# An attention and gated feed-forward kernel on one core: LayerNorm sums of one block moved to ScalarE, a new start, a new schedule, and the last store in two parts

## The chip, the core and the metric

The kernel runs on one core of one Trainium2 chip. The metric is device time in microseconds (us), quoted as the median of a kernel's runs; lower is better. The profiled span is shorter than the time of the same run by about 1.7 us (560.1 and 561.8 for the kernel before), so spans are compared with spans and times with times.

## The reference, cut to what matters

```python
S, D, H, W, F = 2048, 576, 32, 256, 4608          # one sequence, bf16
xn = layernorm(x)                                 # no scale, no shift, eps 1e-5
q, k, v = split(xn @ wqkv)                        # 32 heads of 18
s = softmax(where(0 <= i - j < W, q k^T * 18**-0.5, -1e9)) v @ wo
h = sigmoid(xn @ w_gate) * (xn @ w_up)            # 576 -> 4608
g = silu(h @ w_down)                              # 4608 -> 576
return x + s * g
```

## The kernel before

A Python program lists operations with engine, estimated duration and dependencies. A list scheduler then orders them per engine, using those estimates alone. So a constant in an estimate moves instructions without changing any of them. The sequence is worked off in four chunks of 512 tokens. The parts that matter:

```python
NTAIL = 96
NWARM = (11, 4, 1)                   # warm-up pairs of 512 columns
PARTS = (((0, 1), (1, 2), (2, 3), (3, 4)),) * 2   # first two feature tiles: block by block of 128 tokens
SPACE_NS = 1500.0                    # least distance of two score groups
BLOCKS = (range(KB), range(1, KB))   # KB = 5: block 0 is the 64-row remainder of D = 576, first in its turn

def turn(eng, outs, lhs, rhs, hi):   # half of a product: first half hi=0, second half hi=1 (array halves swapped)
    for k in BLOCKS[hi]:
        res = pair(eng, outs, ..., not hi and k == 0, bool(hi) and k == KB - 1, hi)

def dve_ns(n, rate=1.0):             # estimate for VectorE
    return n / (0.96 * rate) + 140.0

# LayerNorm of block i (build_ln)
b1 = op("DVE", 390, ... bn_stats(columns 0:288));  b2 = op("DVE", 390, ... bn_stats(columns 288:576))
ag = op("DVE", 200, ... bn_aggr);  ve = op("DVE", 140, ... add EPS)
rs = op("POOL", 560, ... pow(-0.5))
ap = op("DVE", 430, ... (x - mean) * rstd);  dup = op("DVE", 180, ... copy of 64 columns)
# ... transposes on TensorE, copy out of PSUM on ScalarE (blocks 0 to 2) or VectorE (block 3)

# last block of the last chunk: 192 columns a half first, then the narrow group of NTAIL a half
self.build_final(sb + 1, hs[1], fa, 0, na)
self.build_final(sb + 1, ht, down(i + 1, ht, 1, [lb], 2 * na, NTAIL), 2 * na, NTAIL)
...
if c0 + w == D:                      # one store of 128 x 576 when both parts are ready
    o = self.dma(self.out[rows, :], self.xf[:, sx, :], ...)

# the sync queue, when the program is written out
for o in self.prog[e]:
    if e == "SP" and o is self.prog[e][-1]:     # ahead of its last DMA
        for i, n in enumerate(lane_cnt):
            if n > 0 and i not in outs:
                eng.wait_ge(lanes[i], n)        # every DMA lane but the output's: 31 instructions in the trace
```

The softmax here doesn't subtract the row's maximum and nothing guards it: scores larger than these inputs give would overflow.

Of the kernel before, what the change touches and what calls it, by code (L numbers as in the profile page):

```python
# [38 lines left out]
TURN_NS = 290.0  # L39
# [6 lines left out]
BINS0 = (((-4, 0, 1), (1, 1, 5), (6, 6, 2)),  # L46
         ((-2, 2, 1), (3, 3, 5)),
         ((0, 0, 5), (5, 5, 3)),
         ((2, 2, 5), (7, 7, 1)),
         ((4, 4, 4),))  # L50
MASKS0 = (((0, 2, 0, 2),), ((2, 1, 0, 2), (7, 1, 0, 1)), ((0, 1, 1, 2), (4, 1, 0, 2)), ((2, 1, 1, 2), (6, 1, 0, 2)), ((4, 1, 1, 2),))
# [6 lines left out]
NTAIL = 96  # L58
NWARM = (11, 4, 1)
NEARLY = 2  # L60
FIRST_SLACK_NS = -970.0
PARTS = (((0, 1), (1, 2), (2, 3), (3, 4)),) * NEARLY
XPRIO = 0
# [6 lines left out]
SHARE_NS = 300.0  # L70
# [5 lines left out]
SPACE_NS = 1500.0  # L76
# [25 lines left out]
BLOCKS = (range(KB), range(1, KB))  # L102
# [10 lines left out]
def turn(eng, outs, lhs, rhs, hi):  # L113
    res = None
    for k in BLOCKS[hi]:
        res = pair(eng, outs, lambda r, t: lhs(r, t, k), lambda r, t: rhs(r, t, k), not hi and k == 0,
                   bool(hi) and k == KB - 1, hi)
    return res


def dve_ns(n, rate=1.0):
    return n / (0.96 * rate) + 140.0
# [54 lines left out]
class Op:  # L177
    __slots__ = ("eng", "est", "deps", "fn", "name", "prio", "start", "end", "tok", "needs_tok",
                 "nbytes", "slack", "idx", "succs", "cidx", "odeps", "acq", "lane", "filler")

    def __init__(self, eng, est, fn, name, deps, prio, nbytes, odeps, acq):
        self.eng = eng
        self.est = float(est)
        self.fn = fn
        self.name = name
        self.deps = []
        seen = set()
        stack = list(deps)
        while stack:
            d = stack.pop(0)  # L190
            if d is None:
                continue
            if isinstance(d, (list, tuple)):
                stack = list(d) + stack
            elif id(d) not in seen:
                seen.add(id(d))
                self.deps.append(d)
        self.prio = prio
        self.start = None
        self.end = None  # L200
        self.tok = None
        self.needs_tok = False
        self.nbytes = nbytes
        self.idx = -1
        self.succs = []
        self.cidx = -1
        self.odeps = [d for d in odeps if d is not None]
        self.acq = acq
        self.lane = None
        self.slack = 0.0  # L210
        self.filler = None
        for d in self.odeps:
            assert d.eng == eng
# [22 lines left out]
class Builder:  # L236
# [38 lines left out]
    def alloc_memory(self):  # L275
# [49 lines left out]
        self.small, _ = seq("small", [P, 3 + 16 * NST], f32)  # L325
# [4 lines left out]
        self.veps = sm[:, 3 + 14 * NST:3 + 15 * NST].rearrange("p (s c) -> p s c", c=1)  # L330
        self.rstd = sm[:, 3 + 15 * NST:3 + 16 * NST].rearrange("p (s c) -> p s c", c=1)
# [62 lines left out]
    def load_x(self, c, i=0):  # L394
        if c == 0:
            for i in range(BPC):
                self.x_dma[i] = (self.dma(self.x0[:, i, :], self.x[i * P:(i + 1) * P, :], P * D * 2, f"dma:x{i}", ("x0", i), prio=XPRIO * (i > 1)),
                                 self.x0[:, i, :])
                self.x_dma[i][0].slack = -220.0
            return  # L400
        st = c * BPC + i
        slots, dd = [], []
        for _ in range(2):
            s_, d_ = self.r_xr.produce()
            slots.append(s_)
            dd += d_
        assert slots[1] == slots[0] + 1
        o = self.dma(self.xr[:, slots[0]:slots[0] + 2, :],
                     self.x[st * P:(st + 2) * P, :].rearrange("(t p) d -> p t d", p=P),
                     2 * P * D * 2, f"dma:x{st}", ("x", slots[0]), deps=[dd, self.hm[6] if c == 1 else None], prio=5)  # L410
        o.slack = 5000.0
        for j in range(2):
            self.x_dma[st + j] = (o, self.xr[:, slots[j], :])
# [5 lines left out]
    def load_rem(self, dst, srcs, name, lane, prio, deps=()):  # L419
        return [self.dma(dst[ROWS[t], :], src[0:RD, :], RD * src.shape[1] * 3, name, lane + (t,), deps=deps, prio=prio)  # L420
                for t, src in enumerate(srcs)]

    def build_consts(self):
# [15 lines left out]
        self.warm(NWARM[0], z, None, 427)  # L439
# [12 lines left out]
        for t in range(2):  # L452
            for i in range(2):
                self.op_wqk4.append(op("DVE", 130, lambda e, t=t, i=i: e.tensor_copy(
                    self.wq4[ROWS[t], 0, i, :], self.wqkr[ROWS[i], 512:D]), f"init:wq4:{t}{i}", deps=self.op_wqk, prio=2))

    def warm(self, n, dep, before, est):
        h, zero = self.warm_h, self.warm_src

        def f_warm(eng):  # L460
            return pair(eng, self.halves(h, NT), lambda r, t: zero[r, :],
                        lambda r, t: zero[r, None, :].broadcast_to([SW, NT // P, P]), True, True)
# [29 lines left out]
    def build_ln(self, c):  # L492
# [3 lines left out]
        for i in range(BPC):  # L496
            st = c * BPC + i
            if c and i % 2 == 0:
                self.load_x(c, i)
            pr = 2 if c else (0, 3, 8, 8)[i]  # L500
            o_x, x_in = self.x_dma[st]
            ss, ds = self.r_st.produce()
            b1 = op("DVE", 390, lambda e, ss=ss, x_in=x_in: e.bn_stats(self.bnst[:, ss, 0, :], x_in[:, 0:288]),  # L503
                    f"ln:bn1:{st}", deps=[o_x, ds], prio=pr)
            b2 = op("DVE", 390, lambda e, ss=ss, x_in=x_in: e.bn_stats(self.bnst[:, ss, 1, :], x_in[:, 288:576]),  # L505
                    f"ln:bn2:{st}", deps=[o_x, ds], prio=pr)
            ag = op("DVE", 200, lambda e, ss=ss: e.bn_aggr(self.mv[:, ss, :], self.bnst[:, ss, :, :]),
                    f"ln:ag:{st}", deps=[b1, b2], prio=pr)
            ve = op("DVE", 140, lambda e, ss=ss: e.tensor_scalar(self.veps[:, ss, :], self.mv[:, ss, 1:2], EPS, None,
                                                                ALU.add), f"ln:ve:{st}", deps=[ag], prio=pr)  # L510
            rs = op("POOL", 560, lambda e, ss=ss: e.tensor_tensor(self.rstd[:, ss, :], self.veps[:, ss, :],
                                                                  self.neghalf[:, :], ALU.pow),
                    f"ln:rs:{st}", deps=[ve, self.op_negh], prio=pr)
            sn, dn = self.r_xn.produce()
            ap = op("DVE", 430, lambda e, ss=ss, x_in=x_in, sn=sn: e.tensor_scalar(  # L515
                self.xnr[:, sn, RD:XW], x_in, self.mv[:, ss, 0:1], self.rstd[:, ss, :],
                ALU.subtract, ALU.mult), f"ln:ap:{st}", deps=[rs, ag, dn], prio=pr)
            dup = op("DVE", 180, lambda e, sn=sn: e.tensor_copy(self.xnr[:, sn, 0:RD], self.xnr[:, sn, RD:2 * RD]),
                     f"ln:dup:{st}", deps=[ap], prio=pr)
# [16 lines left out]
            if i < 2:  # L536
                self.warm(NWARM[1 + i], None, tr, 216)

# [3 lines left out]
            eng = "DVE" if i == 3 else "ACT"  # L542
            xe = op(eng, dve_ns(KB * P, 1.9) if i == 3 else act_ns(KB * P), f_xe, f"xe:{st}", deps=[tr], prio=0)
            h.release(xe)
            self.op_xnT[c].append(xe)

# [111 lines left out]
    def build_attn(self, c, hg):  # L658
# [21 lines left out]
        for vi, (specs, groups) in enumerate(zip(bins, masks)):  # L680
# [15 lines left out]
            self.last_vis = sc  # L696
            vis.append(sc)
# [34 lines left out]
    def build_pv(self, c, pr):  # L732
# [5 lines left out]
        kss = [ks for ks in (0, 5, -4, -3, -2, -1, 1, 2, 3, 4, 6, 7) if c or ks >= 0]  # L738
# [25 lines left out]
        for i in range(2):  # L764
# [10 lines left out]
            rc = op("DVE", 200, lambda e, o1=o1: e.reciprocal(o1[:, :, DH], o1[:, :, DH]), f"rc:{c}:{pr}:{i}", deps=[t1], prio=1)  # L775
# [55 lines left out]
    def build_ffn(self, c):  # L831
# [17 lines left out]
        def weights(wg):  # L849
# [5 lines left out]
            if wg % 2 == 0:  # L855
# [4 lines left out]
                                                ("wgr", sr), pr, [dr])  # L860
            ds += self.op_wgr[wg - wg % 2]
            slots[wg] = sw
            wops[wg] = ds
            if c == 0 and wg == 0:
                for d in ds:
                    d.slack = FIRST_SLACK_NS
# [11 lines left out]
        def gate_up(ft, h, half, acq, part=None, deps=()):  # L878
# [8 lines left out]
            def f(eng):  # L887
                return turn(eng, [bank(h, w)[:, t0:t0 + n] for w in range(2)], lhs, lambda r, t, k: x_in[r, k, t0:t0 + n], half)
            o = op("PE", len(BLOCKS[half]) * mm_ns(n), f, f"f1{half}:{c}:{ft}", deps=[xin, wops[ft // WG], deps],
                   prio=3 if part is None else 1, odeps=chain[half] if part is None else [], acq=acq)  # L890
# [16 lines left out]
        early = NEARLY if c == 0 else 0  # L907
        if early:
# [3 lines left out]
            for ft, h in enumerate(hs):  # L912
                u = None
                for part in range(len(PARTS[ft])):
                    lo = gate_up(ft, h, 0, None if part else h, part, [u])
                    u = gate_up(ft, h, 1, None, part, [lo])
# [3 lines left out]
        for ft in range(early, NFT):  # L920
            if ft % WG == 0 and ft // WG not in slots:
                weights(ft // WG)
            h = self.pool_f.hold()
            lo = gate_up(ft, h, 0, h)
# [30 lines left out]
        for i in range(0, BPC, 2):  # L955
# [7 lines left out]
            ht = self.pool_s.hold()  # L963
# [5 lines left out]
            lb = down(i + 1, ht, 0, [], 2 * na, NTAIL)  # L969
            fa = down(i + 1, hs[1], 1, [la], 0, na, range(NFG - 1, NFG))  # L970
            self.build_final(sb + 1, hs[1], fa, 0, na)
            self.build_final(sb + 1, ht, down(i + 1, ht, 1, [lb], 2 * na, NTAIL), 2 * na, NTAIL)
        self.prev_f2_last = new_last

    def build_final(self, sb, h, f2, c0=0, n=288):
# [42 lines left out]
        if c0 == 0:  # L1018
            self.fq3 = []
        self.fq3.append(q3)  # L1020
        if c0 + w == D:
            o = self.dma(self.out[rows, :], self.xf[:, sx, :], P * D * 2, f"dma:out:{sb}", ("out", sx), deps=self.fq3, prio=2)
            self.r_xf.release(sx, o)

    def schedule(self):
# [14 lines left out]
        while nsched < len(ops):  # L1040
            best = None
            for e in ENGS:
# [4 lines left out]
                if e == "PE":  # L1047
                    for o in cand:
                        if o.acq is not None:
                            due = last_sc + SPACE_NS if o.name.startswith("sc") else 0.0  # L1050
                            claims.setdefault(o.acq.pool.name, []).append((o.prio, o.cidx, max(ready_t[o.cidx], due)))
                bk = None
                for o in cand:
                    st = max(free[e], ready_t[o.cidx])
                    early = 0.0
                    if e == "PE" and o.name.startswith("sc"):
                        early = min(max(0.0, last_sc + SPACE_NS - st), FILL_NS)
# [24 lines left out]
            if o.name.startswith("sc"):  # L1082
# [24 lines left out]
            for s_ in o.succs:  # L1107
# [8 lines left out]
                if remaining[s_.cidx] == 0:  # L1116
# [121 lines left out]
```

## Time and profile before

| | kernel before |
|---|---|
| time, three runs | 562.5 us (562.21 to 562.64) |
| profiled span | 560.1 |
| all matmuls but the warm-ups at their steady rates | 542.5 |
| first gate/up matmul | 7.87 |
| the 144 small (128-column) gate/up matmuls done | 12.89 |
| TensorE's last matmul ends | 556.27 |
| last store issued, landed | 557.89, 559.64 |

The table cuts the span into three: a start (to 12.89), a middle (12.89 to 556.27, 543.38 us), and an end (3.84 us).

### The profile page before, as it was taken

How to read it: one execution, taken by the hardware profiler on the slowest of the kernel's cores; microseconds unless marked ns; L12 is line 12 of the kernel's file. 1: busy time of each engine (PE TensorE's matmuls, PEld its weight loads, DVE VectorE, ACT ScalarE, POOL GpSimd, SP SyncE). 2: the span in 40 equal slices, each digit the busy share in tenths (PEclk: the TensorE clock that was granted, in tenths of full speed). 3: DMA queues.
4: the chain of work that ended last, by engine and by line, in shares of the span. 5: the costliest groups of instructions: out<-in, count | busy, mean ns of one | idle time of the engine just before them, and what ended most of it. 6: DMA issues, size and time to landing. Idle time of an engine off the chain costs nothing.

```text
span 560.1 us, 19180 instructions
## 1 busy us (share of the span) xinstructions
PE 553.5 (99%) x8300; PEld 335.7 (60%) x8300; DVE 335.7 (60%) x793; ACT 271.4 (48%) x379; POOL 210.8 (38%) x358
## 2 busy tenths in 40 slices
PE   8999999999999999999999999999999999999997
PEld 4454544677764454556877566555487754444786
DVE  5576879769587776734886773586656133333133
ACT  3245655545655656466655636665754133323011
POOL 4564467473366534405674530465330100000000
PEclk9999999999999999999999999999999999999999
DMA  8975899541215454427321243454521126552010
GB/s 230 319 216 153 241 279 261 154 59 35 76 37 155 133 143 144 116 75 128 97 58 35 81 116 98 125 157 125 164 66 36 32 70 176 166 161 57 1 44 23
DMA packets 113323, 67.81 MB, mean 121 GB/s; under 512 B 18476, under 2 KB 111372, under 8 KB 113240
## 3 DMA queue, kind: packets, MB, share of 16 engines
q1 hardware_dynamic: 105816, 60.68, 39.6%
q0 software_dynamic: 7424, 5.92, 3.9%
q8 instruction: 65, 1.06, 0.8%
q14 instruction: 18, 0.15, 0.1%
HBM read 55.15 MB, written 2.36 MB: 103 GB/s over the span
## 4 chain that ended last, share of the span: by engine, by line
PE 97%; DVE 2%; DMA 0%; issue 0%; DVEq 0%
PE ps L109 93%; PE ps L754 3%; DMA x<-in_A_x_dram 0%; DVE o2T L780 0%; DVE ot L772 0%; DVE small L503 0%; DVE s_attn L1005 0%; DVE small L505 0%; DVE o L776 0%; DVE thf L1010 0%; DVE v_aug L652 0%; DVE xnr L515 0%; PE ps L553 0%; DVE xf L1015 0%; DVE ot L775 0%
## 5 line engine op out<-in xcount | busy, mean ns | idle before, releaser
L109 PE MATMUL ps<-xnT,wgs 64*128 64x512 bf16 (+1 forms) x2400 | 285.6, 368 | 0.1
L704 ACT ACTIVATE expr<-ps 128x1024 bf16<-128x1024 f32 (+2 forms) x160 | 156.7, 979 | 86.6 <-PE ps L109 86.0
L109 PEld LDWEIGHTS ps<-xnT,wgs 64*128 64x128 bf16 x2400 | 113.8, 94 | 116.8 <-PE ps L109 0.9
L109 PE MATMUL ps<-wd_sb,hT 64*128 64x288 bf16 (+2 forms) x2448 | 154.3, 276 | 0.0
L900 DVE SCALAR_TENSOR_TENSOR hT<-tring,ps 128x512 bf16<-128x512 bf16 x144 | 98.0, 683 | 89.6 <-ACT tring L897 87.1
L897 ACT ACTIVATE tring<-ps 128x512 bf16<-128x512 f32 x144 | 85.9, 597 | 114.4 <-PE ps L109 112.7
L109 PEld LDWEIGHTS ps<-wd_sb,hT 64*128 64x128 bf16 x2448 | 113.1, 94 | 28.0
L265 POOL DMA_DIRECT2D qk<-qd x160 | 82.6, 524 | 106.6 <-PE ps L109 99.8
L717 DVE TENSOR_TENSOR expr<-expr,mask 128x256 bf16<-128x256 bf16 (+2 forms) x232 | 63.7, 305 | 53.2 <-ACT expr L704 52.5
L669 POOL TENSOR_SCALAR kx<-kprev,small 128x256 bf16<-128x256 bf16 x64 | 62.0, 979 | 31.5 <-PE ps L109 30.8
L265 POOL DMA_DIRECT2D oT<-o2T x72 | 36.9, 520 | 61.9 <-DVE o2T L780 50.0
L109 PE MATMUL ps<-qk,kx 64*128 64x320 bf16 (+4 forms) x736 | 59.8, 251 | 0.0
L109 PE MATMUL ps<-xnT,wgr 64*128 64x512 bf16 (+1 forms) x300 | 55.9, 368 | 0.3
L109 PEld LDWEIGHTS ps<-qk,kx 64*128 64x128 bf16 x736 | 32.0, 94 | 25.5 <-DVE hT L900 1.4
L109 PE MATMUL ps<-xnT,wqk 64*128 64x512 bf16 x256 | 32.6, 377 | 0.0
L772 DVE STREAM_TRANSPOSE ot<-ps 128x512 f32<-128x512 f32 x32 | 22.4, 701 | 13.4 <-PE ps L754 13.3
L995 ACT ACTIVATE thf<-ps 128x576 bf16<-128x576 f32 (+3 forms) x22 | 11.4, 519 | 36.3 <-PE ps L109 35.8
L591 DVE CAST qd<-ps 128x1024 bf16<-128x1024 f32 (+1 forms) x20 | 22.2, 1114 | 6.2 <-PE ps L109 5.9
L669 DVE TENSOR_SCALAR kx<-qk,small 128x512 bf16<-128x512 bf16 x64 | 22.2, 373 | 3.3 <-PE ps L109 3.1
L780 DVE STREAM_TRANSPOSE o2T<-o 128x512 bf16<-128x512 bf16 x32 | 22.8, 711 | 1.1
L109 PEld LDWEIGHTS ps<-xnT,wgr 64*128 64x128 bf16 x300 | 15.0, 94 | 13.8 <-issue 1.3
L825 ACT ACTIVATE s_attn<-ps 128x576 bf16<-128x576 f32 x16 | 9.9, 648 | 27.1 <-PE ps L109 27.1
(64 smaller groups left out, 301.9 us busy)
## 6 DMA issues: line engine op xcount, KB each, us to landing
wgs<-in_B_w_gate_dram SPq DMA_DIRECT2D x72, 256.0 KB, 3.4
wgs<-in_B_w_up_dram SPq DMA_DIRECT2D x72, 256.0 KB, 3.9
wd_sb<-in_B_w_down_dram SPq DMA_DIRECT2D x9, 576.0 KB, 6.4
qk<-qd POOLq DMA_DIRECT2D x100, 36.0 KB, 2.3
wgr<-in_B_w_gate_dram SPq DMA_DIRECT2D x36, 64.0 KB, 2.3
wgr<-in_B_w_up_dram SPq DMA_DIRECT2D x36, 64.0 KB, 2.4
xf<-in_A_x_dram SPq DMA_DIRECT2D x16, 144.0 KB, 2.7
out_dram<-xf SPq DMA_DIRECT2D x16, 144.0 KB, 1.8
```

The costliest lines, as they stand in the source:

```text
L109: res = eng.matmul(outs[i], lhs(ROWS[t], i), rhs(ROWS[t], i), start=start, stop=stop, tile_position=(64 * t, 0))
L265: o = self.op(eng, DMA_ISSUE_NS[eng], lambda e: e.dma_start(dst, src), name, deps, prio, nbytes=nbytes)
L591: return eng.tensor_copy(dst, self.both(h, n))
L669: return e.tensor_scalar(self.kx[:, sx, pos:pos + n_ // SW, t, :], src.rearrange("p (s k) -> p s k", k=SW), self.half[:, t:t + 1], None, A ...
L704: return eng.activation(self.expr[:, se, :, lo * SW:NT], self.both(h, NT)[:, :, lo * SW:NT], ACTF.Exp, scale=SM_SCALE)
L717: return eng.tensor_tensor(e_, e_, m_, ALU.mult)
L754: res = eng.matmul(outs[i][p0:p0 + VH, cols], self.v_aug[ROWS[i], o:o + VH], self.expr[ROWS[i], se, t, cols], start=n == 0, stop=n == len( ...
L772: return e.transpose(self.ot1[:, p1, :], self.halves(hp, NT)[i])
L780: t2 = op("DVE", dve_ns(NT), lambda e, p2=p2, p3=p3: e.transpose(self.o2T[:, p3, :], self.o2[:, p2, :]), f"ot2:{c}:{pr}:{i}", deps=[on, d3 ...
L897: th = op("ACT", act_ns(NT), lambda e: e.activation(self.tring[:, st, :], bank(h, 0), ACTF.Tanh, scale=0.5), f"th:{c}:{ft}", deps=[pg, dt_ ...
L900: mu = op("DVE", dve_ns(NT), lambda e: e.scalar_tensor_tensor(self.hT[:, ft, :], self.tring[:, st, :], 1.0, bank(h, 1), ALU.add, ALU.mult) ...
L995: return e.activation(v2(t)[:, a:b, :], y2()[:, a:b, :], ACTF.Tanh, scale=0.25)
```

## The change

The intent: shorten the start (ScalarE, idle there, takes the sums of block 2; short warm-ups; the remainder's weights last, so that the first turn waits for two loads only), drop the score columns of the first chunk that only meet keys before the sequence, give the scheduler numbers nearer to measured ones, and let the last block's first part be stored while the second is computed. The order of the P V products became a named list with the same content.

```diff
+STATS_ACT = (2,)
-NWARM = (11, 4, 1)
+NWARM = (43, 10)                       # pairs of 128 columns now
-NTAIL = 96
+NTAIL = 112
-BLOCKS = (range(KB), range(1, KB))
+BLOCKS = ((1, 2, 3, 4), (1, 2, 3, 4, 0))
-BINS0 = (((-4, 0, 1), (1, 1, 5), (6, 6, 2)), ((-2, 2, 1), (3, 3, 5)), ...)
+BINS0 = (((0, 0, 5), (5, 5, 3)), ((1, 1, 5), (6, 6, 2)), ...)   # no negative key blocks in chunk 0
-TURN_NS = 290.0
+TURN_NS = 265.0
-SHARE_NS = 300.0
+SHARE_NS = 0.0
-SPACE_NS = 1500.0
+SPACE_NS = ((1500, 1500, 1400, 1500, 2000, 1200, 2000, 1100), ...)   # per chunk and head group
-    return n / (0.96 * rate) + 140.0
+    return n / (0.96 * rate) + 160.0
@@ build_ln, block 2 of chunk 0
+        a1 = op("ACT", ..., activation(junk, x_in, Identity, accum_out=sx))
+        m  = op("POOL", ..., nm = sx * (-1 / D))
+        a2 = op("ACT", ..., activation(junk, x_in, Square, bias=nm, accum_out=sq))
+        v  = op("POOL", ..., ve = sq / D + EPS)
+        rs = op("POOL", ..., pow(-0.5))
@@ build_ffn, chunk 0
+   the first half turn of feature tile 2 (512 columns) is placed inside tile 1's last parts as filler
@@ build_final
-        if c0 + w == D:
-            o = self.dma(self.out[rows, :], ...)
+        if c0 == 0 or c0 + w == D:
+            a, b = self.out_from, c0 + w
+            o = self.dma(self.out[rows, a:b], ...)
```

(Cut: the reciprocal's estimate 200 to 255, slacks and priorities of loads, mask tables, bookkeeping.)

## The prediction

> **What bounds the kernel now.** I read the page's engine shares first, then the chain of waits, then the start, one middle stretch and the end in the timeline, because the page already says that the middle is full.
>
> ```profile
> span 560.1 us, 19180 instructions
> PE 553.5 (99%) x8300; PEld 335.7 (60%) x8300; DVE 335.7 (60%) x793; ACT 271.4 (48%) x379; POOL 210.8 (38%) x358
> PE 97%; DVE 2%; DMA 0%; issue 0%; DVEq 0%
> ...
> 24.14 2.75 PE L109 MATMUL ps<-xnT,wqk 64*128 64x512 bf16 x24
> 26.73 0.38 PE L109 MATMUL ps<-xnT,wgr 64*128 64x512 bf16 x2
> ```
>
> TensorE is busy 99% and is 97% of the chain. Busy alone could hide slow matmuls, so I check the rate: 24 matmuls of 512 columns run as 12 pairs (two 64-row halves of the array at once), and the next group starts 26.73 - 24.14 = 2.59 us later, 0.216 us a pair. I did this for every group, from the start times of the 8300 matmuls: 0.216 us a pair at 512 columns, 0.123 at 288, 0.056 at 128, 0.028 at 64. Counting all matmuls but the warm-ups at these rates (P V as eight at a time) gives 542.5 us. The rest of the 560.1 us is what any change to the schedule can win: 7.87 us before the first gate/up matmul, 3.84 us after the last matmul, and some 6 us of small holes between[...].
>
> The start (timeline of TensorE, VectorE):
>
> ```profile
> 1.05 3.90 PE L109 MATMUL ps<-hT 64*128 64x512 bf16 x22 [1.05 <-DVE small L434]
> 5.72 0.32 PE L553 MATMUL ps<-ident,xnr 64*128 64x64 bf16 x10 [0.76 <-DVE xnr L518]
> 7.33 0.32 PE L553 MATMUL ps<-ident,xnr 64*128 64x64 bf16 x10 [0.43 <-DVE xnr L518]
> 7.49 0.38 PE L109 MATMUL ps<-hT 64*128 64x512 bf16 x2
> 7.87 0.23 PE L109 MATMUL ps<-xnT,wgr 64*128 64x128 bf16 x2
> 9.85 0.43 DVE L515 TENSOR_SCALAR xnr<-x,small 128x576 bf16<-128x576 bf16 x1 [0.66 <-POOL small L511]
> 12.88 0.38 PE L109 MATMUL ps<-xnT,wgr 64*128 64x512 bf16 x2
> ```
>
> Real work starts at 7.87, behind one left-over 512-column warm-up pair and behind the weights: the four loads of the first weight group land at 6.33, 7.32, 7.52 and 7.74 (the 64-row remainder last). From 7.87 to 12.88, 5.01 us, TensorE does 144 matmuls of 128 columns (72 x 0.056 = 4.03) and two transposes (0.30): 0.68 us of holes, waits for the normalised blocks, which come off one VectorE chain some 1.6 us apart.
>
> A hole in the middle, and the end:
>
> ```profile
> 130.41 0.10 PEld L109 LDWEIGHTS ps<-wvr,xnT 64*128 64x128 bf16 x2 [0.40 <-DVE v_aug L652]
> ...
> 554.78 0.81 DVE L1005 TENSOR_TENSOR s_attn<-s_attn,ps 128x192 bf16<-128x192 bf16 x2 [2.20 <-PE ps L109]
> 556.23 0.36 DVE L1015 TENSOR_TENSOR xf<-xf,thf 128x384 bf16<-128x384 bf16 x1
> 557.53 0.26 DVE L1015 TENSOR_TENSOR xf<-xf,thf 128x192 bf16<-128x192 bf16 x1
> 552.61 5.62 SPq L265 DMA_DIRECT2D out_dram<-xf  x2
> L1157 SPq EVENT_SEMAPHORE  x31: 28/28/28, 553.0 to 554.8; - x31
> ```
>
> The last store is issued at 557.89, lands at 559.64, and the span ends at 560.11. The last line is the one that matters for the change: before the last store the sync queue takes 31 wait instructions, one for every two DMA lanes, which stand in the program only ahead of its last DMA. They run from 553.01 to 554.88, 61 ns each, and cost nothing now, since the store before them went out at 552.61 and the last one's data is ready only at 557.79.
>
> [...]the first warm-up pairs start 0.427 us apart, and from about 3.9 us on 0.216. [...]each P V group starts about 0.09 us late and the next group about 0.15 us late. [...]the 128x512 tanh took 0.60 us here[...]. [...]the 144 KB store landed in 1.75 us, of which its packets moved for about 0.5.
>
> **The change part by part.**
>
> *Third block's sums on ScalarE.* VectorE loses two statistics passes (0.45 + 0.44), the aggregate (0.20) and the add (0.15) of block 2. ScalarE gains two 576-column passes[...], at a time when it idles (from 2.3 to 6.1 us); GpSimd gets two small operations. Block 2 lands at 4.16, [...]its inverse root, behind block 1's on GpSimd, near 7.4. VectorE, in the built order, then goes straight from block 1 (7.27) to normalise block 2: ready near 8.1 instead of 8.88. Block 3: near 9.75 instead of 10.49.[...]
>
> *Warm-ups of 128 columns, remainder last.* 43 pairs: about 25 cold at 0.107 and 18 warm at 0.056 end near 4.8, as now. The gain is that ten short pairs (0.56) fit wholly between the two transposes and none follows the second. The 64-row remainder block moves from first to last in its turn, so the first gate/up turn needs only the loads that land at 7.32. It can start at 7.49 instead of 7.87: 0.38 us. Counting on in the built order with the readiness above (transposes of block 2 near 8.2, of block 3 near 9.8), I find one hole of about 0.1 in place of 0.68, and the 144 small matmuls are worked off at about 11.95 instead of 12.88: **-0.93 us**. (A first half of the third feature tile now stands inside them as filler, which I take out of the count.)
>
> *No zero blocks.* Score columns of the first chunk: 736 matmuls become 704. 16 pairs x 0.029 = **-0.47 us** on TensorE. ScalarE's exp gets 256 columns less a head group (8 x 0.21 = 1.7 us), beside TensorE, so worth nothing.
>
> *The new order.* A turn's second half that directly follows its first waits 0.23 us. Counting by the built order, the old one exposes 0.23 + 0.13 + 0.07 + 0.07 = 0.50, the new one 0.23 twice: -0.03. The hole of 0.26 at 130.41 (a V projection waiting for VectorE) has one 288-column down group more ahead of it, 0.49 us: **-0.26**. Another of 0.28 near 327.6 keeps its pattern, and I leave it. P V: the order is the same list, so 0. For holes that a new order makes I add **+0.2**.
>
> *Last store in two, 112 columns.* Let B be the start of the last narrow group (554.58 before). It has 36 pairs, 0.0493 instead of 0.0427 us each[...], so TensorE ends at B + 1.94 instead of B + 1.69. VectorE's first part, 1.81 us, loses 1.04 ns a column: 1.73, done at B + 1.93, so the second part no longer queues. That is the intent, and alone it would put the last store at B + 3.54. But the 31 lane waits still stand ahead of the last DMA, and now the first half of the store stands ahead of them: issued B + 2.03, + 0.34 for its issue, + 0.06, + 31 x 0.0605 = 1.88, + 0.07: the last store goes out near **B + 4.38**. It is 56 KB instead of 144; with 0.3 us less to move it lands in about 1.45. End: B + 4.38 + 1.45 + 0.47 = B + 6.30, 4.36 after TensorE's end instead of 3.84: **+0.52 us**. Without the lane waits it would have been 0.32 less than now.
>
> Sum: -0.93 - 0.47 - 0.03 - 0.26 + 0.2 + 0.52 = -0.97 us. From 562.5: **561.5 us**.
>
> **The rivals.**
> 1. The lane waits do not bite (the half store goes out earlier, or the waits pass faster). For it: they are satisfied long before. Against: they took 61 ns each though satisfied, and the queue is in order. It would be 560.7.
> 2. ScalarE's two sums are slower or late, for instance a separate read-out of the accumulator: then its copy of block 0 comes after 7.4 us and the first turn waits, or GpSimd's chain of three keeps block 2 back. Half the start's gain is lost: 562.0.
> 3. The new order opens new holes: VectorE holds PSUM banks behind transposes, as at 130.41 and 327.6, and the feed-forward work is spread otherwise over chunks. Four or five holes of 0.3 give 562.7. For it: VectorE is at 90% and more in some slices. Against: the old order had only two such holes of over 0.2 us after 14 us.
> 4. The new order has fewer: the estimates of VectorE's times were raised towards what the trace shows. 0.3 off the holes near 327 and the last small ones: 561.0.
> 5. Weights come late, as TensorE is about 0.9 us earlier. Against: the second group lands at 9.54 and 10.38, needed near 11.7; the third at 12.25, needed after 14.
>
> **Range and chances.** The start is worth 0.5 to 1.1, the order between -0.6 and +0.8, the end between -0.3 and +0.8; together a little over 0.9 either way. The runs before differ by 0.4. So 560.4 to 562.4. A gain of 2% is 11 us[...]; a loss of 2% would need a wait that repeats all through the kernel. Both get 1%.
>
> **What would show it.** Right: first gate/up matmul near 7.5, the 144 small ones done near 12 (filler taken out), 704 score matmuls; the two last stores about 2.35 us apart with 31 waits between; the span ending about 4.4 us after the last matmul; a span near 559.1. Wrong: a first turn after 7.9, the last store right behind VectorE's last result, or idle TensorE over 1 us in all in the middle.

What it rests on, in the trace of the kernel before unless said otherwise:

- "Cold" and "warm" are its words for pairs at the first rate and at the later one: 0.427 and 0.216 us at 512 columns. The cold 0.107 at 128 columns is an estimate, a quarter of 0.427.
- The 16 P V groups account for about 4 of the 6 us of small holes: each starts 0.09 us late, and the products in it and the group behind it take 0.12 to 0.18 longer than at the steady rates. Why is not shown.
- ScalarE took 0.65 us for 576 columns (128x576, out of PSUM); the two passes measured 0.68 and 0.77 in the profile after, without the read-outs. The 7.4 for block 2's inverse root holds, as an estimate from GpSimd's row: block 1's root ends at 6.59 and a root takes 0.55, which leaves 0.26 for the small operation between.
- The second half turn at 14.20 came 0.23 us late (0.23 at 23.16 and 45.70 in the profile after); those given 0.13, 0.07 and 0.07 stood at 94.36, 103.00 and 64.60, 0.12, 0.07 and 0.06 late. ScalarE's exp took 1.022 us for 1024 columns and 0.809 for 768, so 0.21 for 256.
- 0.0493 us at 112 columns is an estimate between 0.0427 at 96 and 0.056 at 128; the profile after has 0.0492. VectorE's 1.04 ns a column: 0.757, 0.557 and 0.357 us for 576, 384 and 192 columns (L1010).
- The 11 us of a 2% gain stand against 17.6 in all (560.1 - 542.5), the start and the end included.

## The result and the profile after

| | before | after |
|---|---|---|
| time, six runs each, same chip and rounds | 562.38 us (561.91 to 562.64) | 560.64 us (560.44 to 560.93) |
| profiled span | 560.1 | 558.9 |
| first gate/up matmul | 7.87 | 7.55 |
| 144 small matmuls done (filler taken out) | 12.89 | 12.35 |
| from there to TensorE's end | 543.38 | 542.15 |
| TensorE's end to the span's end | 3.84 | 4.39 |

The ratio is 0.997 (95% interval 0.9957 to 0.9983). A ratio is the mean time of one kernel's fast runs over that of the other's of the same rounds, so not quite the ratio of the medians. The three parts of the two profiles add up: -0.54 - 1.23 + 0.55 = -1.22, the difference of the spans. The medians differ by 1.74. The profiled run of before (561.84) was quicker than all its six timed runs, so its start is probably a good one.

The page of the changed kernel, first and chain lines, and one line of the DMA queues that I had not read in the page of before (name and kind of queue: packets, MB, share):

```profile
span 558.9 us, 19273 instructions
PE 98%; DVE 1%; DMA 0%; issue 0%; DVEq 0%
...
q8 instruction: 66, 1.08, 0.8%
```

The bound is the same. The last line becomes important in the experiments: 66 packets of 16 KB fit TensorE's program in number: 16,684 matmuls and weight loads, so about 253 in each, some 126 matmuls with their weight loads. (That the queue feeds TensorE is inferred from this count.)

The start of the changed kernel in the timeline (start, duration, engine, line, operation, count; in brackets the idle time before it and what ended it), TensorE first, then ScalarE and VectorE:

```profile
1.05 4.76 PE L121 MATMUL ps<-hT 64*128 64x128 bf16 x86 [1.05 <-DVE small L450]
7.28 0.32 PE L598 MATMUL ps<-ident,xnr 64*128 64x64 bf16 x10 [0.35 <-DVE xnr L544]
7.55 0.95 PE L121 MATMUL ps<-xnT,wgs 64*128 64x128 bf16 x24
12.07 1.25 PE L121 MATMUL ps<-xnT,wgs 64*128 64x512 bf16 x16
...
4.74 0.68 ACT L585 ACTIVATE tring<-x 128x576 bf16<-128x576 bf16 x1 [2.45 <-DMA x<-in_A_x_dram]
5.33 0.19 ACT L585 ACTIVATION_READ_ACCUMULATOR tring<-x 128x1 f32 x1
5.88 0.77 ACT L587 ACTIVATE tring<-x,small 128x576 bf16<-128x576 bf16 x1 [0.36 <-POOL small L586]
6.56 0.19 ACT L587 ACTIVATION_READ_ACCUMULATOR tring<-x,small 128x1 f32 x1
...
7.72 0.43 DVE L540 TENSOR_SCALAR xnr<-x,small 128x576 bf16<-128x576 bf16 x1 [0.50 <-POOL small L589]
```

The first turn now starts with a weight block of the big load (wgs) at 7.55. Each of ScalarE's two sums is followed by a separate instruction that reads its accumulator, 0.19 us. The first sum starts when block 2 has landed, at 4.72; in the kernel before it landed at 4.16. VectorE normalises block 2 at 7.72 (8.24 before).

The stretch of the hole at 130.41 before, in the timeline of the changed kernel's TensorE:

```profile
130.28 0.67 PE L121 MATMUL ps<-wd_sb,hT 64*128 64x288 bf16 x8
130.78 0.65 PE L121 MATMUL ps<-wv_sb,xnT 64*128 64x288 bf16 x8
131.28 0.65 PE L121 MATMUL ps<-wd_sb,hT 64*128 64x288 bf16 x8
```

Four pairs of 288 columns take 0.49 us and the groups start 0.50 apart: the hole is gone.

The end of the changed kernel: VectorE's lines, the sync queue's stores, and its wait instructions (count: shortest, median and longest ns, first and last start):

```profile
554.15 0.34 DVE L1071 TENSOR_TENSOR xf<-xf,thf 128x352 bf16<-128x352 bf16 x1
554.55 0.65 DVE L1061 TENSOR_TENSOR s_attn<-s_attn,ps 128x112 bf16<-128x112 bf16 x2
555.66 0.27 DVE L1071 TENSOR_TENSOR xf<-xf,thf 128x224 bf16<-128x224 bf16 x1
550.60 6.62 SPq L278 DMA_DIRECT2D out_dram<-xf  x3
L1216 SPq EVENT_SEMAPHORE  x31: 28/28/28, 554.9 to 556.8; - x31
```

The three stores of the fourth line go out at 550.60, 554.52 and 556.89 by the trace's single records. The last one's data is ready at 555.66 + 0.27 = 555.93, 0.96 us before it is issued. Between the two stands the row of 31 waits, as predicted.

### The profile page after: what moved, and what is told of

Same layout as the page of the kernel before. It is cut to its first block, busy times and chain, and to the rows that moved or that the text cites. A ratio compares the mean times of both kernels' runs of the same rounds, so it can differ in the third digit from the quotient of the medians.

```text
span 558.9 us, 19273 instructions
## 1 busy us (share of the span) xinstructions
PE 553.0 (99%) x8342; PEld 339.5 (61%) x8342; DVE 333.6 (60%) x797; ACT 274.3 (49%) x383; POOL 210.8 (38%) x360
## 4 chain that ended last, share of the span: by engine, by line
PE 98%; DVE 1%; DMA 0%; issue 0%; DVEq 0%
PE ps L121 94%; PE ps L800 3%; DMA x<-in_A_x_dram 0%; DVE small L524 0%; DVE small L526 0%; PE ps L598 0%; DVE xnr L540 0%; DVE s_attn L1061 0%; DVE thf L1066 0%; DVE xnr L544 0%; DVE small L528 0%; DVE small L530 0%; DVE xf L1071 0%; DVEq L1226 0%
## 5 line engine op out<-in xcount | busy, mean ns | idle before, releaser
L121 PE MATMUL ps<-xnT,wgs 64*128 64x512 bf16 (+1 forms) x2400 | 282.5, 368 | 0.1
L750 ACT ACTIVATE expr<-ps 128x1024 bf16<-128x1024 f32 (+4 forms) x160 | 154.9, 969 | 77.8 <-PE ps L121 77.2
L121 PE MATMUL ps<-wd_sb,hT 64*128 64x288 bf16 (+2 forms) x2448 | 156.7, 276 | 0.0
L763 DVE TENSOR_TENSOR expr<-expr,mask 128x128 bf16<-128x128 bf16 (+2 forms) x240 | 63.6, 298 | 62.0 <-ACT expr L750 61.5
L121 PE MATMUL ps<-qk,kx 64*128 64x320 bf16 (+1 forms) x704 | 59.4, 254 | 0.0
L696 ACT ACTIVATE v_aug<-ps 64x288 bf16<-64x288 f32 x32 | 13.1, 409 | 17.3 <-PE ps L121 16.8
```

What stands on the lines that cost most here:

```text
L121: res = eng.matmul(outs[i], lhs(ROWS[t], i), rhs(ROWS[t], i), start=start, stop=stop, tile_position=(64 * t, 0))
L696: return eng.activation(dst, src, ACTF.Copy)
L750: return eng.activation(self.expr[:, se, :, lo * SW:NT], self.both(h, NT)[:, :, lo * SW:NT], ACTF.Exp, scale=SM_SCALE)
L763: return eng.tensor_tensor(e_, e_, m_, ALU.mult)
```

## The experiments

Two chips were used; each kernel is compared with runs of before, or of its sisters, on the same chip. The text names the runs by their labels: e0 is the changed kernel once more, e1 has the waits first, e2 one store, e3 the sums on VectorE, e4 the zero blocks, e5b the old numbers, e6 the remainder first, e7 is the kernel before once more, e8 and e9 have the 512-column warm-ups, e10 and e11 the shifted program. One caution first. The same kernel submitted as a "new" one (the run e7_before_again, below) came out at 562.88 us against 562.24 of before in the same rounds. So medians of five runs do not establish differences below about 0.6 us; there the parts of the profile decide.

### The changed kernel once more

No edit. 

> The changed kernel unaltered, as the yardstick for the others on this chip. Expected: 560.6 us, 1.7 below the kernel before, a span near 558.9, the last store issued 4.3 us after the last narrow group starts. If its lead over the kernel before were nearer 1.0 here, the 1.7 of the first comparison would have been partly chance.

Measured: 560.94 us (560.43 to 561.36) against 562.18 of before on that chip, ratio 0.9976 (0.9961 to 0.999). Middle 542.16 and end 4.39 repeat to 0.01. The small matmuls were done at 12.45, and there a hole showed that no part of the change accounts for. Timeline of TensorE:

```profile
9.94 0.27 PE L121 MATMUL ps<-xnT,wgs 64*128 64x128 bf16 x3
10.41 0.80 PE L121 MATMUL ps<-xnT,wgs 64*128 64x128 bf16 x21 [0.20 <-issue]
```

A row of 24 equal matmuls is cut after three, and "issue" says that no wait in the profile ended the hole. The third and the fourth are the two halves of one pair: they start 0.42 us apart (pairs elsewhere in this row start both halves within 0.01), and what follows is 0.36 late. I come back to it.

### The lane waits ahead of the first half of the store

```diff
-                if e == "SP" and o is self.prog[e][-1]:
+                if e == "SP" and o is self.prog[e][-2]:
```

> The 31 lane waits are moved ahead of the last but one DMA of the sync queue, nothing else. Theory (the waits stand between the two half stores and hold the last one): the last store goes out 0.1 us behind VectorE's last result, 0.8 us earlier than in the changed kernel, and the time falls by 0.8 to near 559.8. Rival (the last store waits for something else, such as the half store before it or VectorE): no change, 560.6.

Measured: 560.06 us (559.5 to 560.32), ratio 0.9958 (0.9945 to 0.997), 0.88 below the run above on the same chip. The waits of this kernel, and VectorE's last result:

```profile
L1216 SPq EVENT_SEMAPHORE  x31: 27/28/28, 551.4 to 553.2; - x31
556.02 0.28 DVE L1071 TENSOR_TENSOR xf<-xf,thf 128x224 bf16<-128x224 bf16 x1
```

The waits run while VectorE still works on the first part. The last store goes out at 556.33, right behind its data (556.30), and the end is 3.45 after TensorE's in place of 4.39. Nothing else in the program moved. This is the cause of the longer end, shown. By its parts it is the best version; its median is level with that of the next run (560.04).

### One store in place of two

```diff
-        if c0 == 0 or c0 + w == D:
+        if c0 + w == D:
```

> The last block is stored whole again, as in the kernel before; all else as changed. Theory (splitting put the waits on the path, and is a loss as built): the store of 144 KB goes out near 3.5 us after the last narrow group starts and lands in 1.75 instead of 1.55, so the time falls by 0.6 to near 560.0. Rival (the split itself is the gain it was meant to be): it rises by 0.2 to 0.3.

Measured: 560.04 us (559.89 to 561.0), ratio 0.9963 (0.9949 to 0.9977). The end is 3.74: the store goes out when its data is ready (VectorE's last result ends at 556.52, store issued at 556.62) and lands 1.75 us later. The half store of the run above lands in 1.54. As built, the split costs 4.39 - 3.74 = 0.65 us; with the waits moved it gains 3.74 - 3.45 = 0.29. The median does not show the difference between 3.74 and 3.45, because starts vary by more. The profiled run had the largest of the holes without a wait:

```profile
10.90 0.80 PE L121 MATMUL ps<-xnT,wgs 64*128 64x128 bf16 x21 [0.64 <-issue]
```

### Block 2's sums back on VectorE

```diff
+    def sums_back(self):        # after scheduling; all other orders stay as built
+        b1, b2 = bn_stats of columns 0:288 and 288:576 of block 2 on VectorE, in the place of block 3's
+        ag, ve = bn_aggr and add on VectorE behind the copy of block 1, block 3's two bn_stats behind them
+        rs = pow on GpSimd;  ScalarE's two passes and GpSimd's two small operations are taken out
```

> The third block's sums go back to VectorE, with the order of all other instructions on all engines frozen as in the changed kernel. Theory (the sums on ScalarE bring blocks 2 and 3 earlier and that is on the path at the start): block 2 ready near 8.8 instead of 8.4, block 3 near 10.4 instead of 10.0, and the time rises by 0.3 to 0.5 to near 561.0. Rival (TensorE is held at the start by the weights alone): no change within 0.1.

Measured: 561.11 us (561.08 to 561.19), ratio 0.9978 (0.9965 to 0.999). The transposes of blocks 2 and 3 stand at 8.99 and 10.60; in the changed kernel at 8.32 to 8.43 and 9.79 to 10.04. So the move to ScalarE brings the two blocks forward by some 0.6 us, as planned. The time rose by only 0.17 over its neighbour e0, less than the 0.3 to 0.5 that I expected and less than medians establish here. (Its first gate/up matmul stood at 7.81, as its second weight load landed at 7.68; 7.19 to 7.41 in the changed kernel's two profiles. The edit does not account for that.) The small matmuls end at 12.85, and this run had no hole at matmul 221: that it was later may be why, which was not tested. What ScalarE's sums win, the hole (0.36 in e0, 0.80 in e2) partly takes back.

### Warm-ups of 512 columns, without and with the moved waits

```diff
-NWARM = (43, 10)
+NWARM = (11, 4)
@@ warm
-            return pair(eng, self.halves(h, P), ..., lambda r, t: zero[r, :], True, True)
+            return pair(eng, self.halves(h, NT), ..., lambda r, t: zero[r, None, :].broadcast_to([SW, NT // P, P]), True, True)
```

> The warm-ups have 512 columns again (11 pairs and 4 pairs), still none behind the second transposes; all else in the order of the changed kernel. Theory ([...]the changed kernel's traces show a hole of 0.1 to 0.9 us at matmul 221 of the program, without any semaphore, just after the second 16 KB instruction packet): with 76 fewer matmuls ahead, matmul 221 falls among 512-column work, no hole stands before it, the small matmuls end near 12.2 instead of 12.35 to 12.95, and the time is 0.2 to 0.5 below the changed kernel's 560.6 to 560.9, near 560.4. Rival (the hole is the weights' or VectorE's): it stays near 10.4 us, time unchanged. The change's own intent would have the 128-column warm-ups gain: then the time rises.

> The 512-column warm-ups of e8 together with the lane waits ahead of the last but one store (e1). If the two causes are separate their gains add: 0.8 to 0.9 from the waits and 0.2 to 0.5 from the warm-ups, near 559.6; a span near 557.8. If either was a chance of its runs, no better than e1's 560.1.

Measured: 561.26 us (561.01 to 562.32) and 560.34 us (559.86 to 560.76), against 562.25 of before on that chip. The waits are worth 0.92 again. The first expectation fell: the time was no better. But the hole did a telling thing. With 76 fewer matmuls in the warm-ups it stood at 13.54 and 13.70, three microseconds later, in front of the last of the small matmuls, yet again in front of matmul 220 of TensorE's program (counted from 0):

```profile
13.54 0.23 PE L121 MATMUL ps<-xnT,wgr 64*128 64x128 bf16 x2 [0.34 <-issue]
```

The trace's records of queue q8 fit. The second packet came at 7.60 to 8.91 where the hole ended at 10.41, at 8.45 to 9.51 where it ended at 10.90, and here at 11.10 to 12.16. TensorE goes on 1.3 to 1.5 us after the packet has ended, in all six profiles with such a hole. The profiles without a hole agree: there the packet had ended 1.28 us or more before matmul 220 started (1.28 in the profile after and in e4, 1.43 in before). My new theory was that the hole belongs to the place in the program, a packet boundary (the "fetch theory" in the text of e11_more_warm_waits). (The text of e10_more_warm says "five of eight profiles". It was six of the ten at that time: e0, e1, e2, e6, e8 and e9.)

### The zero blocks back

```diff
+                if c == 0 and vi in (1, 3):      # two more 64-column matmuls a group, results overwritten
+                    res = pair(eng, [b[:, 0:SW] for b in outs], ..., True, True)
```

> The zero blocks' matmuls come back in TensorE alone: in two of the five score groups of each head group of the first chunk one pair of 64 columns is added, which writes PSUM columns that nobody reads; the order of all else is the changed kernel's. Theory (TensorE is full in the middle, each matmul removed counts whole): the time from the end of the small matmuls at the start to TensorE's end grows from 542.16 by 16 x 0.029 = 0.47 to 542.6, the run by 0.5 to near 561.3. Rival (the score groups wait for ScalarE or VectorE anyway): 542.2, unchanged.

Measured: middle 542.61 in place of 542.16, +0.45 for 16 pairs. That is within 0.02 of the predicted 0.47. The time, 561.09 (560.86 to 563.01), lies within the noise of the sisters.

### The remainder first, as before

```diff
-BLOCKS = ((1, 2, 3, 4), (1, 2, 3, 4, 0))
+BLOCKS = ((0, 1, 2, 3, 4), (1, 2, 3, 4))        # first half turns wait for the remainder's loads too
```

(Cut: the remainder's rows swapped to match, and lines that keep the order as built.)

> The 64-row remainder block goes first in a turn again, as in the kernel before, in the frozen order of the changed kernel. Theory (its loads land last, at 7.6 to 7.9, and hold the first gate/up turn): the first gate/up matmul starts near 8.0 instead of 7.5; as the second half turn of the changed kernel waits for the same loads near 8.05, only 0.1 to 0.3 us of it reaches the end of the small matmuls, and the time rises by 0.1 to 0.3. Rival (the blocks' normalisation bounds the start, not the weights): no change.

Measured: 561.35 us (561.12 to 561.91), ratio 0.9979 (0.9966 to 0.9993). The first turn, in the timeline of TensorE:

```profile
7.86 0.23 PE L121 MATMUL ps<-xnT,wgr 64*128 64x128 bf16 x2 [0.22 <-DMA wgr<-in_B_w_up_dram]
```

It waits for the remainder, which landed at 7.73, and starts 0.36 later than in e0, e1 and e2 (7.50). That was predicted as 0.38. The middle grew by 0.64, which I had not expected; 0.6 of it are three holes of 0.16 to 0.25, ending at 91.8, 232.6 and 317.9 us; a fourth, of 0.20, ends at 35.7. I put them down to the new lengths of half turns (10 and 8 matmuls in place of 8 and 10, in an order built for 8 and 10), which is argued, not tested. So the time of this run is not the worth of the remainder's place alone.

### The program shifted by 46 matmuls

```diff
-NWARM = (43, 10)
+NWARM = (66, 10)
-        self.warm(NWARM[0], z, None, 107)
+        self.warm(NWARM[0], z, None, 67, 80)     # the first 66 pairs with 80 columns
```

> The changed kernel with 66 first warm-up pairs of 80 columns in place of 43 of 128, nothing else: the same stretch of time, but every later matmul of TensorE's program stands 46 places further on. My theory: the hole without a semaphore, seen before matmul 220 or 221 in five of eight profiles, belongs to the place in the program[...]. Here [...]matmul 221 is the 49th or so after the second transposes, and the next boundary, 349, lies behind the 144 small ones. So: no hole without a semaphore between 7.5 and 13, the small ones done at 11.8 to 12.1 (12.35 and 12.45 in two profiles of the changed kernel), and the time 0.2 to 0.5 below the changed kernel's, near 560.3 to 560.7. Rival A: the hole hangs on the time or on what stands there, so it stays near 10.4 to 10.9 us, and the time is the changed kernel's, 560.6 to 560.9. Rival B: shorter warm-ups leave the clock cold or delay the first transposes: they would start after 5.8 and everything would be later by that.

(The boundary at 349 is an estimate: 221 and 128 matmuls, taken near the 126 that 66 packets for 16,684 instructions give.)

> The same with the 31 lane waits ahead of the half store (both mends together, the candidate for a version better than either kernel). If both theories hold the gains add: end minus TensorE's end 3.45, small ones done at 11.8 to 12.1, time 0.9 below e10_more_warm, 559.4 to 559.8, and below e1_waits_first's 560.06. If the fetch theory falls: 559.9 to 560.2, the same as e1_waits_first.

Measured: 562.45 us (561.25 to 564.37) and 561.33 us (560.38 to 563.92), against 562.24 of before on that chip. Neither is better than its partner without the shift (560.94 and 560.06 on the other chip): both are worse, by 1.3 to 1.5 us. Rival B as written is refuted: the first transposes started at 5.62 and 5.72, and the granted clock had risen at 4.56 and 4.69. Two causes show, one in each profile.

The second of the two had no hole at 220, as the theory said. It had one 128 matmuls further on, at the next packet boundary, 348, and the longest of all:

```profile
13.35 0.59 PE L121 MATMUL ps<-xnT,wgs 64*128 64x512 bf16 x4
15.28 0.60 PE L121 MATMUL ps<-xnT,wgs 64*128 64x512 bf16 x4 [1.34 <-issue]
```

Its third packet started at 12.90 and ended at 13.91; TensorE went on 1.37 later, and the hole cost 1.5 us. So the place of the hole is settled: 220 or 221 in six of fourteen profiles, 348 in one, nowhere else, whatever stands there. What makes a packet start is not settled. The second starts when 130 to 180 matmuls have started. The third comes at 12.7 to 13.8 us in all ten profiles with the new start and small warm-ups, with 248 to 334 matmuls started, so it does not follow the matmuls' number alone. My forecast that boundary 349 would be harmless rested on that, and failed. Its small matmuls were done at 12.49, not 11.8 to 12.1; the first turn had waited for weights until 7.96.

The first profile had another trouble. In this run the last three loads of the first weight group landed late (8.82 to 9.29; 7.0 to 8.2 in the sisters with normal warm-ups), and TensorE idled. Two lines of TensorE's timeline, then the table of windows (stretch, length, busy times with counts; TensorE's granted clock stands in the third number from the end):

```profile
7.26 0.32 PE L598 MATMUL ps<-ident,xnr 64*128 64x64 bf16 x10 [0.76 <-DVE xnr L544]
8.96 1.47 PE L121 MATMUL ps<-xnT,wgs 64*128 64x128 bf16 x24 [1.38 <-DMA wgs<-in_B_w_up_dram]
...
7.00:9.00 2.00, 0.36 (x12) 0.28 (x14) 1.06 (x5) 0.70 (x1) 0.94 (x2) 0.74 0.92 257
9.00:11.00 2.00, 2.00 (x45) 2.00 (x47) 0.87 (x9) 0.17 (x1) 1.20 (x3) 0.50 0.82 231
11.00:13.00 2.00, 2.00 (x43) 2.00 (x40) 0.00 (x0) 0.54 (x1) 1.94 (x2) 0.50 1.08 290
```

The granted clock rose at 4.56, fell to half at 7.97 and rose again at 14.80 by the trace's clock records; in between the pairs of 128 columns start 0.107 apart in place of 0.056. The small matmuls were done at 16.09. What made the clock fall is not shown. The fall came 3.41 us after the rise, and TensorE had been busy for 1.83 of them; in the second profile it was busy for 1.90 of the 3.41 us after the rise at 4.69, and the clock stayed up. That the short warm-ups made TensorE idle is not shown either: they ended at 5.03, those of e1 and e2 at 5.10 and 5.14. The next longest run of this kernel and the longest of the second have a lower mean clock as well (563.28 us at 0.995, 563.92 at 0.993). Whether the earlier instruction packet (6.06 to 7.07, and 5.15 to 6.11 in the other) made the weights late, I cannot tell from two profiles.

### The old numbers for the scheduler

```diff
-TURN_NS = 265.0;  SHARE_NS = 0.0;  SPACE_NS = ((1500, 1500, 1400, ...), ...)
+TURN_NS = 290.0;  SHARE_NS = 300.0;  SPACE_NS = ((1500,) * 8,) * 4
-    return n / (0.96 * rate) + 160.0        # and 255 for the reciprocal
+    return n / (0.96 * rate) + 140.0        # and 200
```

> The changed kernel with the scheduler's numbers of before: even spacing of the score groups (1500 ns), TURN_NS 290, SHARE_NS 300, 140 ns for VectorE's overhead, 200 for the reciprocal. The program's instructions are the changed kernel's, in another order. Theory: the order's gain of 0.76 us comes from these estimates and the hand-set spacing, so it is lost: half turns that follow their first halves directly expose 1.30 us by the built order (0.58 in the changed kernel), and holes for VectorE come back. TensorE's end minus the end of the small ones 542.9 to 543.9 (542.16 in the changed kernel), time 561.3 to 562.5. Rival: the gain comes with the new head groups of the first chunk and the start, whatever the numbers: 542.1 to 542.5, time 560.6 to 561.2.

Measured: 563.35 us (563.24 to 563.56), ratio 1.0017 (1.0003 to 1.003): slower than the kernel before. The middle is 544.73, 2.57 above the changed kernel's, more than I expected. Excess over the steady rates, by kind of group: 1.90 against 0.24 at score groups, 2.44 against 1.75 at gate/up groups, 0.87 against 0.63 at down groups (from the start of a group to the start of the next). One of the holes in TensorE's timeline:

```profile
88.46 0.35 PE L118 MATMUL ps<-qk,kx 64*128 64x320 bf16 x4
89.06 1.04 PE L118 MATMUL ps<-xnT,wgs 64*128 64x512 bf16 x8 [0.24 <-DVE hT L945]
```

The two score pairs, one of 320 columns and one of 128 (the line shows the first's shape), should take 0.19; the gate/up turn behind them starts 0.60 later, because VectorE still reads the PSUM bank that it needs (hT). The rival, that the gain comes from the new program whatever the numbers, is refuted. Set against the kernel before without its zero blocks (543.38 - 0.47 = 542.91), the new instructions lose 1.82 with the old numbers and gain 0.76 with the new. Five constants were set back at once, the hand-set spacing among them; which of them matters was not tested.

### The kernel before once more

No edit. 

> The kernel before, unchanged, for a second profile: how much do the terms that I compare vary by themselves? I expect TensorE's end minus the end of the small ones within 0.05 of 543.38, end minus TensorE's end within 0.1 of 3.84, and the small ones done between 12.7 and 13.4 (12.89 in the profile of before, whose run of 561.84 was quicker than the six timed ones). If the first term moves by 0.3 or more, the 0.76 that I give to the order is not established.

Measured: 562.88 us (561.6 to 563.56); its profile's run was its quickest, 561.60. Middle 543.39 (543.38) and end 3.83 (3.84): these parts are as firm as clockwork, and so are the differences read from them. The start is not: small matmuls done at 12.64 (12.89). Both profiled runs of before are among its quickest, so its usual start is probably later than either shows.

## Why the prediction was right, point by point

The time fell inside the range (560.64 predicted as 560.4 to 562.4) and within 2% of before. Its centre, 561.5, was 0.9 too high. By its own steps:

- **The start, -0.93: the first turn right, block 2 too early, the sum too large.** Measured -0.54 from the profile pair. Over the first four profiles with this start (12.35, 12.45, 12.71, 12.94) and the two of before (12.89, 12.64) it is only -0.15. The first turn is where predicted (7.55; "near 7.5"), and e6_rem_first shows why. The term that was mis-sized is the readiness of blocks 2 and 3. Predicted transposes: near 8.2 and 9.8; measured 8.43 and 10.04. The step behind it is "Block 2 lands at 4.16", read from one profile: it landed at 4.72 here, at 4.30 to 4.83 in the eleven other profiles of changed kernels, and at 4.51 in the second profile of before. The sums themselves were not slow: from the landing to the inverse root 2.97 us passed, 3.24 by the forecast. The read-out of the accumulator that rival 2 feared exists (0.19 us after each pass), but the forecast had room for it, and ScalarE's copy of block 0 started at 6.65, not after 7.4. The two holes before the transposes make 0.20 of the 0.40 between 11.95 and 12.35; the rest is the first turn (0.06) and smaller ones. Beside that stands what the prediction did not know at all: in three of those four profiles a hole of 0.30 to 0.80 without a wait, at a packet boundary of TensorE's instructions. The new start reaches matmul 221 at about 10 us, 3 us earlier than before.
- **The warm-ups.** "25 cold and 18 warm end near 4.8" was wrong in the profile after. All 43 ran at 0.107 to about 5.6 us, and the clock rose only at 6.5. In the fourteen profiles the last pair at half speed ended anywhere between 3.6 and 6.9, whatever the kernel (4.87 and 3.59 in the two of before). Since block 0's transposes stand at 5.6 to 5.7 in all of them, this cost little.
- **Zero blocks, -0.47: right.** 0.45 when put back.
- **The order, -0.03 - 0.26 + 0.2 = -0.09: mis-sized.** Measured -1.23 + 0.47 = -0.76, firm to 0.01 in both kernels' second profiles. The hole at 130.41 went, as predicted. The one near 327, which I left in place, went too. And the allowance of +0.2 for new holes met none. Rival 3 (new holes) was wrong and rival 4 (estimates nearer to the trace) right in kind: with the old numbers the same program would have lost 2.57. I gave rival 4 only 0.3.
- **The end, +0.52: right.** Measured +0.55; the last store was predicted at B + 4.38 and came at 556.89, B + 4.32, with B = 552.57. It landed in 1.55 (1.45 predicted; its packets moved for 0.32 in place of 0.55, so the smaller store saved 0.2 and not 0.3). Moving the waits gave back 0.94, and 0.39 less than before remained (predicted 0.32). Rival 1, waits that do not bite, is refuted.
- **What stays open.** The parts of the profiles explain 1.2 of the 1.74 between the medians. The remainder may lie with the run-to-run start of the kernel before; that is not shown, as both its profiles are of quick runs. What makes an instruction packet start is open as well.

The sum -0.97 came close to the -1.22 of the spans because two errors cancelled: the start gave 0.4 less than planned, the order 0.67 more.

## What to carry to other kernels

Waits that were long satisfied still took their turn on the sync queue here, 61 ns each, and held the store behind them (31 of them, 1.9 us; with them moved ahead in e1 the end was 0.94 us shorter). So before splitting a transfer, look at what stands between the two halves in the program, and move it to where the queue idles anyway. In a kernel that is bound by one engine, the numbers that the scheduler works with, estimates and hand-set spacing, decide as much as the instructions: here the same new instructions took 2.6 us longer with the old numbers, more than the whole change gained (1.7). So test them apart. A landing time read from one profile is one draw: block 2's load varied from 4.16 to 4.83 us. And cut the trace into start, middle and end before comparing: the middle and the end repeated to 0.01 us, while the medians of the same kernel differed by 0.6.
